# One choice of experts per batch, the threshold ahead of constants, and raised lengths in the planner of an attention and mixture-of-experts kernel

## The chip, the cores and the metric

The kernel runs on one core of a Trainium2 chip. The metric is the device time of one execution, in microseconds (us). Of the kernel before, three runs took 615.66, 617.41 and 619.67 us; the median is 617.41 us.

## The reference

Attention over 4 batches of 8 heads, with 576 rows of 64 elements in each, feeds a layer of 8 experts. A score counts only if it lies within `tau` of its row's largest.

```
scores = scale * np.matmul(q, k.transpose(0, 1, 3, 2))
thresh = np.max(scores, axis=-1, keepdims=True) - tau
scores = np.where(scores >= thresh, scores, -1000000000.0)
...
attn = attn / (np.sum(attn, axis=-1, keepdims=True) + 1e-09)
...
x = attn_out.transpose(0, 2, 1, 3).reshape(2304, 512)
logits = x @ w_gate                      # 512 x 8
expert_idx = np.argmax(logits, axis=1)
gate_w = softmax(logits)[n, expert_idx]
for i in range(N):                       # first come, first served: capacity 576 per expert
    if counts[e] < capacity: disp[e, counts[e]] = x[i]
...
h = np.maximum(np.einsum('ecd,edf->ecf', disp, w1), 0.0)     # w1 512 x 1024
y = np.einsum('ecf,efd->ecd', h, w2)                          # w2 1024 x 512
out[i] = gate_w[i] * y[expert_idx[i], pos[i]]                 # 0 where not kept
```

## The kernel before, in words

**Tiling.** The 32 heads are worked as 16 pairs, four pairs to a batch. A head's 576 rows are four blocks of 128 and a tail of 64 (`TAIL`). For each pair q and k are loaded, scaled and split into a high and a low half of 16 bits (L773 on ACT, L780 on POOL, the first pair's L782 on DVE) and transposed by DMA. TensorE computes the scores `s` (L846), DVE takes row maxima (L873, L875), TensorE computes the transposed scores `d` (L846), ACT the exponential (L938), DVE keeps what is above the threshold (L942), ACT makes the high half (L908), POOL the low half (L912), and TensorE multiplies by v (L958, L970) into `xo`. ACT copies that to `xs` (L985), DVE forms the reciprocal `rc` of the sums (L991, L992), and POOL scales the rows into `xr`, and those of the tail into `xrt` (L1006). For the x = 0 and x = 1 heads of a pair this covers 128 rows at a time, for x = 2 (both tails) 64.

**Gating.** It is done when a batch's fourth pair is done, and twice: for the four groups of 128 rows (index 0), then for the tail (index `NJ` = 4; its 128 partitions hold two halves of 64 rows). Each time DVE finds the largest logit (`gate1`, L1086, L1087), ACT the exponentials (L1094), DVE the choice of expert `oh` (L1099 to L1104), TensorE the rank of each row within its expert (L1111 to L1118), and DVE the running count `cum` (L1122), the row's metadata (`meta`, L1128 to L1135), and the row index `ixi` to write to (`gate2`, L1140 to L1151). POOL then writes the rows to `xd` in DRAM with indirect DMAs (L1157), four and then one. The next pair's work is mixed in between.

**Experts.** After the third batch the first eight tiles (one to an expert) can be gathered (L364, `earlyy`). After the fourth, the counts are summed (`tot`, L488), a chain of small DVE operations (L491 to L603, among them `gix` L579) finds out which expert each of 13 more tiles belongs to, and POOL gathers these (`latey`). A tile is transposed (`x0`, L373), split (ACT L376, DVE L381), multiplied by w1 (`A`, L399 early, L406 late), passed through the rectifier (L424, L428) and multiplied by w2 (`B`, L445); the results are scaled (L635, L639) and written (L642). The weights are loaded into `ws` (L318) and split by ACT (L329, L331, L332) and by DVE (L336) or POOL (L334).

**What sets the order.** A planner in the kernel (`Plan`) holds every task with an engine, a length in ns, what it waits for, and a priority. It simulates the engines and each time starts the best task that can begin within a window; tasks in `urgent` are taken within another (`HOLD`). The result is a fixed order of instructions for each engine, and each engine runs its own in that order. A task's length thus changes no work, only the order. The tasks `xm`, `xt`, `ta`, `gate1`, `scat` and `tot` of the code are the operations above.

## Time and profile before

| what | value |
|---|---|
| median of three runs | 617.41 us |
| profiled execution | 614.46 us |
| its span | 612.4 us |
| PE busy | 529.5 us, 86% of the span |
| DVE busy | 433.5 us, 71% |
| POOL busy | 446.6 us, 73% |
| ACT busy | 396.5 us, 65% |

The span is the profiled part of the execution; 2.06 us of its 614.46 us lie outside. Busy shares are means over a program with three parts: the attention pairs up to about 350 us, a passage from the last pair to the experts, and the experts from about 390 us on. A table by stretches shows which engine is full in each part.

### The profile page before, as it was taken

Reading aid. Unit: us, or ns where it says so; the run is one execution under the profiler, and the core shown is the slowest. Engines: PE = TensorE matmul, PEld = TensorE weight load, DVE = VectorE, ACT = ScalarE, POOL = GpSimd, SP = SyncE. Lnnn points to the kernel's source line nnn. Section 1 sums busy time; section 2 is a strip of 40 time slices with the busy share of each in tenths; the row PEclk is TensorE's granted clock in tenths of the full one; section 3 lists DMA queues with packets and bytes.
Section 4 is the critical chain, followed back from the end, with each engine's and each line's share of the span. In section 5 each row is a group of like instructions: output and inputs, shape, how many; then the busy total and the mean of one; then the engine's idle time right before and its main releaser. Section 6 shows DMA issues by size and latency. Waiting matters only on the chain.

```text
span 612.4 us, 16304 instructions
## 1 busy us (share of the span) xinstructions
PE 529.5 (86%) x6122; PEld 343.0 (56%) x6122; DVE 433.5 (71%) x999; ACT 396.5 (65%) x551; POOL 446.6 (73%) x382
## 2 busy tenths in 40 slices
PE   2868889887998979997687868699999999999993
PEld 1334545554664646665466744575774687468651
DVE  5886787889897899887776895355555555555652
ACT  5585887897897869896378755356676547625400
POOL 5365967878997689897499446308998868956864
PEclk9897999999999999998798988899999999999997
DMA  6967775578777686872152868754497529643952
GB/s 142 167 123 152 137 155 106 130 105 190 123 151 138 103 205 117 139 106 70 60 155 91 294 190 256 201 65 138 172 232 201 167 84 266 193 169 78 209 179 102
DMA packets 165327, 92.80 MB, mean 152 GB/s; under 512 B 141172, under 2 KB 153528, under 8 KB 165243
## 3 DMA queue, kind: packets, MB, share of 16 engines
q1 hardware_dynamic: 152458, 49.59, 43.0%
q0 software_dynamic: 12352, 41.80, 21.1%
q8 instruction: 53, 0.87, 0.6%
q10 hardware_dynamic: 432, 0.30, 0.2%
q14 instruction: 32, 0.25, 0.1%
HBM read 53.25 MB, written 10.24 MB: 104 GB/s over the span
## 4 chain that ended last, share of the span: by engine, by line
PE 61%; DVE 13%; DMA 11%; ACT 6%; POOL 4%; issue 3%; another core or an unknown queue 1%; SPq 0%; POOLq 0%; ACTq 0%; DVEq 0%
PE b L406 12%; PE s L846 7%; DMA qT<-qn 6%; PE d L846 6%; PE b L399 6%; PE gp L445 6%; PE xo L445 6%; PE xo L958 6%; PE b L445 5%; DVE mx L873 3%; PE xo L970 3%; DMA out_dram<-latey,oix 2%; DVE w2b L942 2%; DVE w1b L942 2%; POOL p L912 2%
## 5 line engine op out<-in xcount | busy, mean ns | idle before, releaser
L873 DVE TENSOR_REDUCE mx<-s 128x1 f32<-128x512 f32 x144 | 95.4, 680 | 26.6 <-PE s L846 25.9
L846 PE MATMUL s<-kT,qT 128*128 128x512 f16 (+2 forms) x576 | 95.8, 306 | 21.1 <-DMA qT<-qn 8.3
L846 PE MATMUL d<-qT,kT 128*128 128x512 f16 (+2 forms) x576 | 88.5, 305 | 10.4 <-DVE w1b L942 4.2
L406 PE MATMUL b<-w1b,latex 128*128 (+2 forms) x816 | 80.7, 276 | 6.9 <-ACT latex L376 3.2
L331 ACT ACTIVATE ws<-ws 128x1024 f32<-128x1024 f32 x48 | 50.5, 1051 | 47.7 <-DMA ws<-in_moe_w_dram 47.7
L406 PEld LDWEIGHTS <-latex 128*128 128x128 f16 (+1 forms) x816 | 63.1, 103 | 23.2 <-issue 6.5
L942 DVE SCALAR_TENSOR_TENSOR w2b<-d,ntau,w2b 128x1024 f32<-128x1024 f32 x56 | 71.4, 1275 | 5.0 <-ACT w2b L938 4.7
L334 POOL TENSOR_TENSOR w1b<-ws,w1b 128x1024 f16<-128x1024 f32 x24 | 51.2, 2142 | 29.8 <-ACT w1b L332 29.6
L912 POOL TENSOR_TENSOR p<-w2b,p 128x1024 f16<-128x1024 f32 x33 | 70.5, 2144 | 2.6 <-DMA qr<-in_q_dram 1.5
L334 POOL TENSOR_TENSOR w2b<-ws,w2b 128x1024 f16<-128x1024 f32 x24 | 51.0, 2137 | 20.5 <-ACT w2b L332 20.3
L938 ACT ACTIVATE w2b<-d 128x1024 f32<-128x1024 f32 x56 | 57.1, 1019 | 12.5 <-PE d L846 12.2
L846 PEld LDWEIGHTS <-qT 128*128 128x128 f16 (+1 forms) x640 | 34.9, 102 | 53.7 <-issue 25.4
L846 PEld LDWEIGHTS <-kT 128*128 128x128 f16 (+1 forms) x640 | 36.6, 101 | 49.9 <-issue 31.1
L445 PEld LDWEIGHTS <-lateh 128*128 128x128 f16 (+1 forms) x408 | 30.7, 103 | 33.8 <-issue 0.8
L958 PEld LDWEIGHTS <-p 128*128 128x128 f16 x1056 | 41.9, 99 | 11.3 <-POOL p L912 1.8
L399 PEld LDWEIGHTS <-w1b 128*128 128x128 f16 x768 | 43.9, 98 | 6.9 <-issue 5.4
L399 PE MATMUL b<-earlyx,w1b 128*128 128x128 f16 x768 | 47.1, 219 | 0.0
L958 PE MATMUL xo<-vH,p 128*128 128x65 f16 x704 | 45.2, 196 | 1.7 <-POOL p L912 1.7
L958 PE MATMUL xo<-vL,p 128*128 128x64 f16 x352 | 41.9, 193 | 0.4 <-issue 0.4
L332 ACT ACTIVATE w2b<-ws 128x1024 f16<-128x1024 f32 x24 | 25.4, 1057 | 21.2 <-PE gp L445 20.6
L318 POOL DMA_DIRECT2D ws<-in_moe_w_dram x50 | 37.4, 751 | 1.2 <-POOL w2b L334 0.9
L908 ACT ACTIVATE p<-w2b 128x1024 f16<-128x1024 f32 x33 | 34.7, 1056 | 0.4 <-DVE w2b L942 0.4
(250 smaller groups left out, 1228.6 us busy)
## 6 DMA issues: line engine op xcount, KB each, us to landing
ws<-in_moe_w_dram POOLq DMA_DIRECT2D x50, 512.0 KB
ws<-in_moe_w_dram SPq DMA_DIRECT2D x14, 512.0 KB
kr<-in_k_dram SPq DMA_DIRECT2D x16, 256.0 KB
qr<-in_q_dram SPq DMA_DIRECT2D x15, 256.0 KB
v<-in_v_dram SPq DMA_DIRECT2D x28, 128.0 KB
kr<-in_k_dram SPq DMA_DIRECT2D x32, 16.0 KB
v<-in_v_dram POOLq DMA_DIRECT2D x4, 128.0 KB
qr<-in_q_dram SPq DMA_DIRECT2D x30, 16.0 KB
```

The lines of the kernel that those rows point to most:

```text
L318: eng.dma_start(out=t, in_=src)
L331: nc.scalar.activation(out=t, in_=t, func=AF.Copy, scale=W_SCALE)
L334: nc.gpsimd.tensor_tensor(out=dst[:, :, 1, :], in0=t, in1=dst[:, :, 0, :], op=ALU.subtract)
L399: nc.tensor.matmul(out=hp[:, f * P:(f + 1) * P], lhsT=wb[0][:, o:o + P], rhs=xT[t][:, xi], start=(d == 0 and z == 0), stop=(d == NB - 1 an ...
L406: nc.tensor.matmul(out=hp[m, 0:FC], lhsT=xT[t][:, xi, m], rhs=wb[0][:, bass.ds(r + (2 * d + wi) * FC, FC)], start=(d == 0 and z == 0), sto ...
L445: nc.tensor.matmul(out=yp[m], lhsT=h[:, o, hi, m], rhs=wb[1][:, bass.ds(r + wi * DM, DM)], start=(z == 0), stop=(z == len(ops) - 1),)
L846: nc.tensor.matmul(out=out, lhsT=l, rhs=r, start=(z == 0), stop=(z == 1), **kw)
L873: V.tensor_reduce(out=m[:, i, 0:1], in_=ps_s[i % 2], axis=AX.X, op=ALU.max)
L912: eng.tensor_tensor(out=p[:, 1], in0=x, in1=p[:, 0], op=ALU.subtract)
L938: nc.scalar.activation(out=t, in_=d, func=AF.Exp, scale=sc_s)
L942: V.scalar_tensor_tensor(out=t, in0=d, scalar=ntau, in1=t, op0=ALU.is_ge, op1=ALU.mult)
L958: nc.tensor.matmul(out=ps_x[:, j * DV:j * DV + r.shape[-1]], lhsT=l, rhs=r, start=(z == 0), stop=(z == len(ops) - 1))
```

## The change

The gating of a batch is done once, with the tail as a fifth group (`NG` = 5): one `gate1`, one choice, one burst of ranks, one `gate2`, and then the five scatters. The tail's transposes and logits come ahead of the last pair's `xt`. `tot` adds the last batch's choices by two further matmuls, and needs only the ranks. The threshold `tau` is handled ahead of most constants and memsets, which become tasks of the planner behind it. The scaling of the x = 2 rows runs on 128 partitions for the later two pairs of a batch, with two small buffers more. A table `FIT` raises planned lengths, five scatters count 1300 instead of 1040, and further tasks are urgent, with priorities ahead of all others. From the diff:

```diff
-    LAND = {"load": 560, "turn": 960, "rows": 2000, "move": 1030, "gather": 980}
+    LAND = {"load": 560, "tau": 2100, "load0": 2300, "turn": 960, "rows": 2000, "move": 1030, "gather": 980}
+    FIT = dict(
+        e={1030: 908, 200: 105}, h16={560: 523, 1030: 948}, hik={1170: 1050}, hiq={1170: 1050}, sck={650: 572}, scq={650: 668},
...
+        m={600: 1280}, max={690: 597, 200: 130}, p={1280: 1190, 200: 190}, r={200: 290}, choice={637: 790, 680: 850}, meta={500: 540, 750: 870},
+        gate1={302: 280, 330: 345}, gate2={650: 860, 900: 1175}, cum={146: 280}, first1={75: 130}, first2={550: 930}, nhi={420: 570}, own={600: 920}, row={150: 260},
...
     def add(self, key, eng, dur, fn, deps, prio, dma=None, kind=None):
+        n = key[0]
+        dur = max(dur, self.FIT.get(n, {}).get(round(dur), dur))
...
-    V.memset(cum, 0.0)
-    V.memset(wg, 0.0)
-    V.memset(zero, 0.0)
...
+    def more_consts(i):
+        if i == 0:
+            V.memset(cum, 0.0)
...
     def emit_tot():
-        nc.tensor.matmul(out=ps_g[:, 512 - E:], lhsT=ones, rhs=cum, start=True, stop=True)
+        oh = gst["oh"]
+        nc.tensor.matmul(out=ps_g[:, 512 - E:], lhsT=ones, rhs=cum, start=True, stop=False)
+        nc.tensor.matmul(out=ps_g[:, 512 - E:], lhsT=ones, rhs=oh[:, NJ + 1], start=False, stop=False)
+        nc.tensor.matmul(out=ps_g[:, 512 - E:], lhsT=ones[0:TAIL], rhs=oh[0:TAIL, NJ], start=False, stop=True)
...
-        xss = [right.tile([P, NJ, D + 2], F32, name=f"xs{i}") for i in range(3)]
+        xss = [right.tile([P, NJ if i < 2 else 2, D + 2], F32, name=f"xs{i}") for i in range(4)]
...
+                if a >= HH // 2:
+                    i, rows = 2 + a % 2, slice(0, P)
+                    t, r1 = xss[i][:, 0:2], rcs[i][:, 1, 0:2]
...
+        def emit_choice(b):
+            V.scalar_tensor_tensor(out=t2, in0=t0, scalar=0.0, in1=dsc(NG, P), op0=ALU.is_equal, op1=ALU.mult)
             V.tensor_reduce(out=fe, in_=t2, axis=AX.X, op=ALU.max)
+            V.tensor_tensor(out=oh[:, 0:NG], in0=dsc(NG, P), in1=bc(fe, NG, P), op=ALU.is_equal)
...
+        T(("pad", 1), "V", 800, lambda: pads(1), [("tau",)], -59)
+        T(("pad", 2), "V", 400, lambda: (pads(2), small_pads()), [("tau",)], -30)
+        T(("const", 0), "V", 1500, lambda: more_consts(0), [("tau",)], -12)
+        T(("const", 1), "V", 1000, lambda: more_consts(1), [("const", 0)], -11)
...
-            T(("ta", qi), "P", 216, partial(emit_turn, b, NJ, 0), [("xm", s - i, 2) for i in range(HH)] + [("lge", b, 1)], t)
-            T(("logit", b, NJ), "P", 756, partial(emit_logit, b, NJ), [("tb", qi), ("gate2", b, 0)], t)
+            T(("ta", b), "P", 216, partial(emit_turn, b), [("xm", s - i, 2) for i in range(HH)] + [("xb", s - 1, 1)], t - 1)
+            T(("logit", b, NJ), "P", 756, partial(emit_logit, b), [("tb", b), ("lwg",)] + last("gate2", b - 1), t - 1)
+            T(("gate1", b), "V", 330, partial(emit_gate1, b), [("logit", b, 0), ("logit", b, NJ)], t)
+            T(("choice", b), "V", 680, partial(emit_choice, b), [("gate1", b)], t)
+            T(("rank", b), "P", 260, partial(emit_rank, b), [("choice", b)] + last("cum", b - 1), t)
+            if b < B - 1:
+                T(("cum", b), "V", 146, partial(emit_cum, b), [("rank", b)], t)
+            T(("gate2", b), "V", 900, partial(emit_gate2, b), [("rank", b), ("meta", b), ("cap",)] + ([("first1",)] if b == B - 2 else []), t)
...
-        T(("tot",), "P", 10, emit_tot1, [("cum", g, NJ), ("gate2", g, NJ)], pt)
+        T(("tot",), "P", 10, emit_tot1, [("rank", g)], pt)
...
+        plan.urgent |= {("av", NPR - 1, x, j) for x in range(3) for j in range(NJ)} | {(n, NPR - 1, c) for n in ("h16", "l16") for c in range(5)}
+        HX = {(n, 0, t) for n in ("h1", "h2") for t in range(NE)}
+        plan.urgent |= HX
+        for k in plan.urgent:
+            if k in plan.tasks:
+                t = plan.tasks[k]
+                plan.tasks[k] = t[:4] + (t[4] / 1000 - (700 if k in HX else 600 if k[0] in ("gate1", "gexp", "choice", "rank", "meta", "gate2", "scat") else 500),) + t[5:]
```

The first place is POOL around the third batch's gating, before: L1157 are the scatters of the four groups (`xr`) and of the tail (`xrt`), L912 low halves of the next pair, L1006 scalings, L794 the low half of v.

```order
L912 TENSOR_TENSOR w1b<-w2b,w1b 128x1024
L1157 DMA xd<-xr,ixi 18432x514 x3
L1006 TENSOR_TENSOR xr<-xs_196,rc_199 128x4x64
L1157 DMA xd<-xr,ixi 18432x514
L912 TENSOR_TENSOR p_160<-w2b,p_160 128x1024
L1157 DMA xd<-xrt,ixi 36864x257
L912 TENSOR_TENSOR p_161<-w2b,p_161 128x1024
L912 TENSOR_TENSOR w1b<-w1b 128x512
```

The same place now (L1171 scatters, L935 low halves, L1033 scalings, L817 v):

```order
L935 TENSOR_TENSOR w1b<-w2b,w1b 128x1024
L1033 TENSOR_TENSOR xr<-xs_180,rc_184 128x4x64
L817 TENSOR_TENSOR vL_151<-v_157,vH_148 128x640
L935 TENSOR_TENSOR p_144<-w2b,p_144 128x1024
L935 TENSOR_TENSOR p_145<-w2b,p_145 128x1024
L935 TENSOR_TENSOR w1b<-w1b 128x512
L1171 DMA xd<-xr,ixi 18432x514
L1171 DMA xd<-xrt,ixi 36864x257
L1171 DMA xd<-xr,ixi 18432x514 x3
```

The five scatters stand in one block, behind three low halves, the scaling and the split of v.

The second place is POOL at the last pair, before (L364 gathers of early tiles, L1006 the last pair's scalings, L1157 the last batch's scatters, L318 loads of weights):

```order
L912 TENSOR_TENSOR p_163<-w2b,p_163 128x1024
L364 DMA earlyy<-xd,gie 128x514 x4
L1006 TENSOR_TENSOR xr<-xs_195,rc_198 128x4x64
L364 DMA earlyy<-xd,gie 128x514
L1006 TENSOR_TENSOR xr<-xs_196,rc_199 128x4x64
L1006 TENSOR_TENSOR xrt<-xs_197,rc_200 64x128
L1157 DMA xd<-xr,ixi 18432x514 x4
L318 DMA ws<-in_moe_w_dram 128x2x512
L1157 DMA xd<-xrt,ixi 36864x257
L318 DMA ws<-in_moe_w_dram 128x2x512
L318 DMA ws<-in_moe_w_dram 128x4x256 x2
L364 DMA latey<-xd,gix 128x514 x6
```

and now (L380 gathers, L1033 scalings, L1171 scatters, L334 loads):

```order
L935 TENSOR_TENSOR p_147<-w2b,p_147 128x1024
L1033 TENSOR_TENSOR xrt<-xs_181,rc_185 128x128
L1033 TENSOR_TENSOR xr<-xs_179,rc_183 128x4x64
L380 DMA earlyy<-xd,gie 128x514 x3
L1033 TENSOR_TENSOR xr<-xs_180,rc_184 128x4x64
L1033 TENSOR_TENSOR xrt<-xs_182,rc_186 128x128
L380 DMA earlyy<-xd,gie 128x514 x3
L1171 DMA xd<-xr,ixi 18432x514
L1171 DMA xd<-xrt,ixi 36864x257
L1171 DMA xd<-xr,ixi 18432x514 x3
L334 DMA ws<-in_moe_w_dram 128x2x512
L380 DMA latey<-xd,gix 128x514 x4
```

The last pair's scaling has no gather in front of it, and one load of weights instead of four lies between the last batch's first scatter and the late gathers.

The third place is DVE in the last batch's gating, before, from the four groups' `gate2` on (L336 splits of w2, L428 and L381 work for early tiles, L491 the first operation of the chain behind `tot`; after these rows the tail's choice, count, metadata and `gate2` follow with four further L336 between them):

```order
L1151 TENSOR_TENSOR ixi<-sm 128x4
L336 SCALAR_TENSOR_TENSOR w2b<-ws,w2b 128x512
L428 SCALAR_TENSOR_TENSOR earlyh<-b_5152,earlyh 128x256
L428 SCALAR_TENSOR_TENSOR earlyh<-b_5153,earlyh 128x256
L1086 TENSOR_REDUCE sm<-gp 128x1
L1087 TENSOR_TENSOR tb<-gp,sm 128x8
L336 SCALAR_TENSOR_TENSOR w2b<-ws,w2b 128x512
L1099 SCALAR_TENSOR_TENSOR tb<-tb,desc 128x8
```

and now (L444 and L397 early tiles, L510 the chain's first, L352 the splits of w2):

```order
L1159 TENSOR_TENSOR ixi<-sm 128x4
L1161 TENSOR_TENSOR sm<-sm 128x1
L1162 TENSOR_SCALAR ixi<-sm,half 128x1
L444 SCALAR_TENSOR_TENSOR earlyh<-b_5157,earlyh 128x256
L510 SCALAR_TENSOR_TENSOR most<-gp,cap_f,fst 128x8
...
L621 TENSOR_TENSOR gix<-own 64x4
L622 TENSOR_TENSOR bad<-own,bl 64x4
L352 SCALAR_TENSOR_TENSOR w2b<-ws,w2b 128x512 x9
```

From `gate1` to the chain's end no split of w2 is left on DVE; nine of them follow behind it.

## Rows read from the trace of the kernel before

**Rows 1.** The page's first part: engine, busy us, share of the span, instructions.
```profile
PE 529.5 (86%) x6122; PEld 343.0 (56%) x6122; DVE 433.5 (71%) x999; ACT 396.5 (65%) x551; POOL 446.6 (73%) x382
```
**Rows 2.** Busy us by stretch: length, engines, granted clock, DMA share, GB/s; cut at pairs' L875.
```profile
126.00:151.00 25.00, 20.21 (x286) 13.05 (x286) 22.86 (x66) 20.24 (x32) 18.85 (x17) 1.00 0.72 148
151.00:168.70 17.70, 15.17 (x223) 9.85 (x222) 14.72 (x32) 14.84 (x22) 17.65 (x15) 1.00 0.76 133
276.70:308.90 32.20, 24.46 (x318) 15.62 (x311) 24.78 (x73) 15.85 (x25) 19.87 (x18) 0.84 0.18 54
...
360.00:400.00 40.00, 27.82 (x162) 17.66 (x162) 22.67 (x89) 15.62 (x31) 22.45 (x24) 0.87 0.75 209
...
460.00:520.00 60.00, 60.00 (x554) 39.31 (x553) 34.42 (x66) 36.23 (x35) 47.96 (x35) 1.00 0.69 183
```
**Rows 3.** Timeline of the start, ACT and DVE: start, length, instruction, idle before and releaser.
```profile
6.96 1.25 ACT L773 ACTIVATE qn<-qr,g 128x1152 f16<-128x1152 f32 x1 [4.65 <-DVE g L296]
6.78 0.15 DVE L296 TENSOR_SCALAR g<-tau_t 128x1 f32<-128x1 f32 x1
```
**Rows 4.** The chain that ended last, first piece: start, length, what.
```profile
1.28 4.25 DMA kr<-in_k_dram
```
**Rows 5.** Timeline of DVE in the third batch's gating.
```profile
281.73 1.27 DVE L1099 SCALAR_TENSOR_TENSOR tb<-tb,desc 128x32 f32<-128x32 f32 x1
283.25 1.82 DVE L1101 TENSOR_TENSOR oh<-desc,sm 128x32 f16<-128x32 f32 x1
...
293.13 2.47 DVE L1099 SCALAR_TENSOR_TENSOR tb<-tb,desc 128x8 f32<-128x8 f32 x1
```
**Rows 6.** Timeline of POOL in the same stretch.
```profile
282.91 2.12 POOL L912 TENSOR_TENSOR w1b<-w2b,w1b 128x1024 f16<-128x1024 f32 x1
287.99 1.03 POOL L1157 DMA_INDIRECT xd<-xr,ixi  x1 [2.97 <-DVE ixi L1151]
...
293.44 2.13 POOL L912 TENSOR_TENSOR p<-w2b,p 128x1024 f16<-128x1024 f32 x1
303.33 0.99 POOL L1157 DMA_INDIRECT xd<-xrt,ixi  x1 [7.76 <-DVE ixi L1149]
```
**Rows 7.** All scatters (L1157): POOL's idle time before them by releaser, us and times.
```profile
  DVE ixi L1149: 8.7, 2
  DVE ixi L1151: 5.4, 3
```
**Rows 8.** Timeline of DVE and POOL at the last pair.
```profile
340.88 0.18 DVE L992 RECIPROCAL rc<-rc 128x4 f32<-128x4 f32 x1
341.58 0.63 POOL L1006 TENSOR_TENSOR xr<-xs,rc 128x256 f32<-128x256 f32 x1
343.45 0.98 POOL L1006 TENSOR_TENSOR xr<-xs,rc 128x256 f32<-128x256 f32 x1
```
**Rows 9.** Timeline of DVE in the last batch's gating.
```profile
353.94 0.18 DVE L1086 TENSOR_REDUCE sm<-gp 128x4 f32<-128x32 f32 x1
354.26 0.68 DVE L336 SCALAR_TENSOR_TENSOR w2b<-ws,w2b 128x512 f16<-128x512 f32 x1
354.86 0.18 DVE L1099 SCALAR_TENSOR_TENSOR tb<-tb,desc 128x32 f32<-128x32 f32 x1
```
**Rows 10.** Timeline of POOL from the last batch's scatters to the late gathers.
```profile
359.17 1.05 POOL L1157 DMA_INDIRECT xd<-xr,ixi  x1 [9.81 <-DVE w2b L336]
...
365.14 1.03 POOL L1157 DMA_INDIRECT xd<-xrt,ixi  x1 [0.30 <-DVE over L620]
370.60 1.07 POOL L364 DMA_INDIRECT latey<-xd,gix  x1 [2.09 <-DVE ex L585]
```
**Rows 11.** Timeline of PE and ACT at the first late tiles.
```profile
374.19 1.46 PE L445 MATMUL b<-w2b,earlyh 128*128 128x512 f16 x6
379.01 1.67 PE L406 MATMUL b<-w1b,latex 128*128 x12 [1.21 <-issue]
389.33 0.38 ACT L424 ACTIVATE hw<-b 128x256 f16<-128x256 f32 x1 [5.17 <-remote]
```

More of the change, by code (lines that the diff above doesn't have):

```diff
@@ L975, in xs_of @@
         def xs_of(s, x):
-            i = (3 * s + x) % 3
+            i = x if x < 2 else 2 + s % HH % 2
             if x < 2:
@@ L1144, in emit_gate2 @@
             )
-            V.tensor_tensor(out=ix, in0=ix, in1=rk, op=ALU.add)
-            if j:
-                V.tensor_tensor(out=dp, in0=ix, in1=dp, op=ALU.add)
-                V.tensor_scalar(out=ixi[:, 0:G], in0=dp, scalar1=2.0, scalar2=half[:, 0:1], op0=ALU.mult, op1=ALU.add)
-            else:
-                V.tensor_tensor(out=ixi[:, 0:G], in0=ix, in1=dp, op=ALU.add)
-            gst[b, j] = (G, n, xrows[b][0 if j == 0 else 1], ixi)
+            for j in (0, NJ):
+                gst[b, j] = (xrows[b][0 if j == 0 else 1], ixi[:, j:])
@@ L1399, in attention_moe_kernel @@
         g = B - 1
[L1400 removed]
+        plan.urgent |= {(n, g) for n in ("gate1", "gexp", "choice", "rank", "meta", "gate2", "ta", "tb")} | {("logit", g, NJ)}
+        plan.urgent |= {("scat", g, 0, r) for r in range(NJ)} | {("scat", g, NJ, 0)} | {(n, g, h) for n in ("lgt", "lge", "lgs") for h in range(2)}
         if PR["urg"] > 0:
```

291 lines of the change are left out of this document (141 added, 150 removed).

## The prediction, made before the changed kernel was run

> **What bounds the kernel now.** I read the page first: PE is busy 86% of the span, no other engine above 73% [rows 1]. That is a mean, so the table of stretches came next [rows 2]. From 460 to 520 us PE is busy 60.00 of 60 us at full clock; such is the whole part of the experts behind its first tiles, and the change leaves that part's matmuls alone. Time can come only from what lies before. There the table shows three kinds of stretch. A pair within a batch takes 17.7 us, with POOL busy 17.65 of it: nothing to take. A pair in which a batch is gated takes 25.0 us (126 to 151; the first two boundaries are alike), with DVE the fullest at 22.86. The third boundary takes 32.2 us, in which no engine is busy above 24.78 and the DMA share is 0.18: there engines wait for each other. And from 360 to 400 us PE is busy only 27.82 of 40. Then I read the timelines of those places, and the waits before POOL's scatters.
>
> **The change, part by part.** The sum is made against the profiled execution, 614.46 us, of which 2.06 lie outside its span. The median of the runs, 617.41, stands 2.95 above it, and I add that at the end.
>
> *Start.* ACT's first scaling waits 4.65 us for `g`, and `g` stands on DVE behind constants and memsets at 6.78 although `tau` was requested first [rows 3]. With those moved behind it, the next thing late is the load: the first chain piece is a load of k in flight from 1.28 to 5.53 [rows 4]. So the gain lies between 0 (later pairs absorb it) and 6.96 - 5.53 = 1.4. The moved operations fall into DVE's idle time before scores exist; if that is not enough they cost what they gave. I take -1.0, near the upper end, because nothing else feeds the first scaling.
>
> *Gating once.* Per batch DVE issues 22 small operations in place of 34 (20 in the last). Two such rows take 354.26 - 353.94 = 0.32 us, or 0.16 each [rows 9], so 12 of them are 1.9 us, on the engine that is fullest at a boundary. The five-group rows are a quarter wider and DVE had 2.1 us idle in the 25.0, so I take -1.2 at each of the first two boundaries: -2.4 (bounds 0 and -3.8). The two more matmuls of `tot` and the longer burst of ranks fall where PE waits for DVE anyway.
>
> *Third boundary.* Here three operations of the two choices took 1.27, 1.82 and 2.47 us [rows 5] where the same take 0.18 in the last batch [rows 9]. Each ends just behind a POOL addition (283.25 + 1.82 = 285.07 against 282.91 + 2.12 = 285.03; 295.60 against 295.57 [rows 5, 6]): they wait for POOL, 5.0 us in all. POOL in turn stood 2.97 and 7.76 us at the scatters for `ixi` [rows 6], with the next pair's low halves behind it in its queue. With one choice and one block of scatters there is one such circle instead of two. The excess over the first boundary is 32.2 - 25.0 = 7.2, and with the 1.2 from above 8.4; I leave one wait of 2.1 behind a POOL addition in the new choice and take -6.3 (bounds 0 and -8.4). The cover is what now stands ahead of the scatters on POOL: three low halves, a scaling and the split of v.
>
> By the Trainium skill (SBUF — State Buffer, section "SBUF: two separate sides"), VectorE and GpSimd share a pair of SBUF ports under an exclusive lock, so that a VectorE operation with two SBUF inputs waits out a GpSimd operation that reads SBUF. The three rows agree with it; by that rule alone the wait belongs to neighbours and not to the number of groups, and the term would be about 2 us smaller with a second wait.
>
> *Last pair.* The second `xr` starts at 343.45 although its `rc` was done at 341.06; ahead of it in POOL's order stand gathers and the first `xr`, at 341.58 [rows 8]. Now the first scaling comes ahead of the gathers and the second waits only for `rc`: up to -2.4. `xt`, the logits and `gate1` hang on it; I take -2.0. The tail's scaling on 128 partitions costs the same columns as on 64; I cost it at nothing.
>
> *From `gate1` to the first late product.* Call G the start of the last `gate1`, 353.94. Before, product A of tile 8 starts at 379.01, G + 25.1 [rows 9, 11]. Twelve splits of w2 lay between on DVE, each 0.60 (354.26 to 354.86), together 7.2, and a second pass of gating; none is left. Reading the new order with the old lengths, `ixi` is ready at about G + 4.6; five scatters at 1.03 + 0.30 [rows 10] end at G + 11.3, against 366.17 = G + 12.2. The first gather came 4.4 us after the last scatter, part of it waiting for the DVE chain. It now starts between G + 11.3 and G + 15.7; I take G + 13.8, against G + 16.7: -2.9. Of four loads of weights between scatters and gathers one is left; with the DMA share at 0.75 and 209 GB/s over this stretch [rows 2], three loads of 512 KB would be 7 us of traffic, and I take -2.0 for the gathers' landing (bounds 0 and -7). That puts the product at G + 20.2, -4.9. The nine splits now behind the chain end at about G + 18.5 and hold B of the early tiles back; one B, 1.46 [rows 11], goes behind as filler and is paid later. Net -3.5 (bounds +2 and -9).
>
> *Raised lengths and new priorities.* They add no work but reorder every engine in every pair. A pair's 17.7 us are POOL's 17.65, so order can hardly gain; where a wait is placed badly it can cost some tenths per pair. I cost it at 0, bounds -3 and +5 (0.3 over 16 pairs).
>
> Sum: -1.0 - 2.4 - 6.3 - 2.0 - 3.5 = -15.2, so 599.3 for a profiled execution, and with 2.95 **602.2 us** for the median. By its own bounds this case runs from 597 to 608. Chance 0.42.
>
> **Rivals.** *More: ACT's stall goes.* At 389.33 ACT had stood 5.17 us before a rectifier, for something the profile calls remote [rows 11]; the chain of rows names no engine of this core. If it hangs on the exact moment or on the traffic there, the shifted order may lose it: 602.2 - 5.2 = 597. Against it: no edit touches what it waited for, as far as the rows show. Chance 0.24.
>
> *Absorbed.* The gain at boundaries is not there: pairs are paced by POOL and DVE's total, and the four groups now wait for the tail's x = 2 rows, so that the early half of the gating no longer overlaps. Then only the start and the passage after G remain: -4.5, which gives 612.9. For it: the first two boundaries have only 1.9 us idle on DVE per 25 to win from. Chance 0.17.
>
> *Slower: POOL's queue blocks at every boundary.* At the first two boundaries all waits for `ixi` together were small: 8.7 - 7.8 = 0.9 for the tail, and of the four groups 5.4 - 3.0 = 2.4 [rows 6, 7]. With the tail in the same `gate2`, the block of five scatters stands on POOL until the tail's logits are done, as the single tail scatter did for 7.76. Two boundaries at 7.8 in place of 3.3 together: +12.3, with no gain at the third, and the start, the passage and the last pair as forecast: 614.5 + 12.3 - 1.0 - 3.5 - 2.0 = 620.3, and 623 to 628 with the 2.95 and a loss by the new order. It decides where the tail's logits come later than POOL's rows ahead of the block, at the third boundary two low halves of 2.1 and a scaling of 0.6 [rows 6, 8], 4.8 us, and two smaller operations; that cover speaks against it. Chance 0.10.
>
> *The new order itself.* Pairs within batches grow by 0.3 us or more each and eat a good part of the 15: 606 to 616. Chance 0.07.
>
> **The numbers.** This kernel's runs spread over 0.65%, so a change under about 1% can't be told from none; the bounds are 611.2 and 623.6. Forecast, ACT's stall, half of the absorbed case, and half of the last one are faster: 0.42 + 0.24 + 0.07 + 0.03 = 0.76. The rest of those two and the lower edge of the slower case are the same: 0.14. Slower: 0.10. The range reaches from 591 (ACT's stall gone and the upper bounds at the boundaries) to 615 (the absorbed case): it leaves out the slower rival and the far low end.
>
> **What would show it.** In the profile after: the first q scaling on ACT at 5.5 to 6, not 7; boundaries of about 24, 24 and 26 us between successive L875 rows, with one wait of POOL before the first scatter of a batch and none before the tail's; choice operations at 0.2, or at most one at 2; the last `gate1` about 12 us earlier than 353.94, from the four terms ahead of it; tile 8's product 20 us after it; then dense PE to the end, as long as before. I am wrong if the pairs within a batch take 18 us or more, if POOL stands over 5 us before each batch's scatters, or if B of the early tiles waits for the nine splits so long that tile 8 comes at G + 25 again.

## The result and the profile after

| kernel | median | runs | before beside it | ratio to before, 95% interval |
|---|---|---|---|---|
| changed | 623.44 us (620.28 to 628.17) | 4 | 616.93 us, 4 runs | 1.0127 [1.0087, 1.0167] |

The change made the kernel 1.3% slower. Forecast were 602.2 us, in a range of 591 to 615, with a chance of 0.10 for slower: the forecast was wrong. The profiled execution took 620.28 us with a span of 618.3, against 614.46 and 612.4. Ratios here and below leave out runs that were over 1.5% above the fastest of their kernel (a slower state); the medians do not.

The page's first part, in the columns of [rows 1]:
```profile
PE 532.3 (86%) x6128; PEld 348.1 (56%) x6128; DVE 432.2 (70%) x950; ACT 398.9 (65%) x547; POOL 447.3 (72%) x382
```
No engine has much more to do (DVE's 49 instructions fewer are the second choice that is gone). What changed is who waits. Stretches of the changed kernel, in the columns of [rows 2]; the cuts are the third boundary (276.77 to 304.93), the last pair up to the last `gate1` (L1101, which I call G, as in the prediction), and the 46.65 us behind G:
```profile
276.77:304.93 28.16, 22.75 (x316) 15.78 (x313) 21.98 (x60) 13.12 (x22) 17.29 (x14) 0.94 0.18 55
304.93:355.45 50.52, 39.30 (x531) 31.40 (x531) 39.59 (x70) 36.75 (x65) 33.37 (x25) 0.83 0.59 189
355.45:402.10 46.65, 30.27 (x243) 21.34 (x242) 24.66 (x98) 17.32 (x36) 22.66 (x23) 0.85 0.58 162
```
The third boundary is 4 us shorter than in [rows 2], the last pair is 5.4 us longer (50.52 against 353.94 - 308.86 = 45.08), and behind G PE works only 30.27 of 46.65 us.

The timeline from the scatters to the first late tiles, of POOL, ACT and PE:
```profile
365.66 0.97 POOL L1171 DMA_INDIRECT xd<-xr,ixi  x1 [0.30 <-issue]
372.76 0.78 POOL L334 DMA_DIRECT2D ws<-in_moe_w_dram  x1 [6.13 <-issue]
373.84 1.06 POOL L380 DMA_INDIRECT latey<-xd,gix  x1 [0.31 <-issue]
...
390.35 1.01 POOL L380 DMA_INDIRECT latey<-xd,gix  x1 [0.30 <-issue]
```
```profile
366.86 0.38 ACT L440 ACTIVATE earlyh<-b 128x256 f16<-128x256 f32 x1 [3.25 <-remote]
392.69 0.38 ACT L440 ACTIVATE hw<-b 128x256 f16<-128x256 f32 x1 [6.57 <-remote]
```
```profile
372.22 0.59 PE L461 MATMUL gp<-w2b,earlyh 128*128 128x512 f16 x1 [7.58 <-DVE w2b L352]
381.18 1.47 PE L422 MATMUL b<-w1b,latex 128*128 x12
394.10 2.83 PE L422 MATMUL b<-w1b,latex 128*128 x12 [5.03 <-ACT hw L440]
```
POOL stands 6.13 us before the one load of weights that was left between scatters and gathers, and all gathers stand behind it. (The row names no releaser. The split of w2 that the load waits for is read from the kernel's dependencies; the first one behind the chain ran on DVE from 371.48, and PE's product that needs it began 0.54 us before the load.) ACT stands twice here for something "remote", where [rows 11] had one such stand of 5.17, and PE stands behind ACT. The last row is also dear in itself: twelve products of 128 columns took 2.83 us there and 1.47 at 381.18. From 392.31 to 399.14 us the granted clock was 0.5 (1.2 GHz), after PE's idle time; at 381 it was 1.0 (2.4 GHz).

**What "remote" is.** The trace also records when each semaphore is raised. I paired the ends of PE's signalling instructions with those records. In the profile of before 582 pairs have a median lag of 0.014 us, but 19 came over 0.4 us late; in the changed kernel it is 32 of 592, up to 8.27 us. Of the 32, 27 overlap the issue of an indirect DMA on POOL (scatters, gathers, outputs), and 4 more begin within 0.6 us of the end of one; of the 19 of before 17 overlap, and 2 begin within 0.6 us. The two stands of ACT above fit two of these signals: matmuls that ended at 363.57 and 384.40 were seen at 366.84 and 392.67, and ACT began 0.02 us later. So PE had finished, and ACT learned of it 3.3 and 8.3 us later. Between 110 and 320 us, where the first three batches' scatters lie, the lags of before sum to 12.3 us (8 signals), those of the changed kernel to 31.2 us (16 signals).

Of ACT, DVE and POOL no signal that has a record came late in either profile. But of the changed kernel's signals 49 have no record (19 of DVE, 18 of ACT, 10 of PE, 2 of POOL), and 47 of these ended in the same places, during or within 0.6 us of an indirect DMA of POOL. So it is not shown that the lag is PE's alone, nor that the recording has no part in it.

### The profile page after: what moved, and what is told of

Read it like the earlier page. It is cut to its first block, busy times and chain, and to the rows that moved or that the text cites. A ratio compares the mean times of both kernels' runs of the same rounds, so it can differ in the third digit from the quotient of the medians.

```text
span 618.3 us, 16259 instructions
## 1 busy us (share of the span) xinstructions
PE 532.3 (86%) x6128; PEld 348.1 (56%) x6128; DVE 432.2 (70%) x950; ACT 398.9 (65%) x547; POOL 447.3 (72%) x382
## 3 DMA queue, kind: packets, MB, share of 16 engines
q1 hardware_dynamic: 152458, 49.59, 40.7%
## 4 chain that ended last, share of the span: by engine, by line
PE 56%; DVE 14%; DMA 12%; POOL 6%; ACT 5%; issue 5%; another core or an unknown queue 1%; SPq 0%; POOLq 0%; DVEq 0%; ACTq 0%
PE b L422 11%; PE d L869 7%; PE s L869 7%; PE b L415 7%; PE xo L981 5%; PE xo L461 5%; PE gp L461 4%; PE b L461 4%; DMA qT<-qn 4%; DVE w2b L965 3%; DMA out_dram<-latey,oix 2%; DVE mx L896 2%; POOL p L935 2%; DVE w1b L352 2%; DMA kT<-kn 2%
## 5 line engine op out<-in xcount | busy, mean ns | idle before, releaser
L869 PE MATMUL d<-qT,kT 128*128 128x512 f16 (+2 forms) x576 | 87.1, 307 | 8.9 <-DVE w2b L965 4.4
L935 POOL TENSOR_TENSOR p<-w2b,p 128x1024 f16<-128x1024 f32 x33 | 70.7, 2147 | 6.5 <-ACT p L931 6.0
L334 POOL DMA_DIRECT2D ws<-in_moe_w_dram x50 | 37.4, 751 | 20.8 <-DVE w2b L352 13.4
L415 PE MATMUL b<-earlyx,w1b 128*128 128x128 f16 x768 | 48.9, 222 | 3.3 <-DVE earlyx L397 3.3
L981 PE MATMUL xo<-vH,p 128*128 128x65 f16 x704 | 47.2, 199 | 4.9 <-POOL p L935 2.8
L981 PE MATMUL xo<-vL,p 128*128 128x64 f16 x352 | 43.3, 196 | 1.0 <-issue 1.0
L444 DVE SCALAR_TENSOR_TENSOR hw<-b,hw 128x256 f16<-128x256 f32 x52 | 22.1, 424 | 20.7 <-ACT hw L440 16.2
```

The source lines that it names most:

```text
L334: eng.dma_start(out=t, in_=src)
L415: nc.tensor.matmul(out=hp[:, f * P:(f + 1) * P], lhsT=wb[0][:, o:o + P], rhs=xT[t][:, xi], start=(d == 0 and z == 0), stop=(d == NB - 1 an ...
L869: nc.tensor.matmul(out=out, lhsT=l, rhs=r, start=(z == 0), stop=(z == 1), **kw)
L935: eng.tensor_tensor(out=p[:, 1], in0=x, in1=p[:, 0], op=ALU.subtract)
L981: nc.tensor.matmul(out=ps_x[:, j * DV:j * DV + r.shape[-1]], lhsT=l, rhs=r, start=(z == 0), stop=(z == len(ops) - 1))
```

## The experiments

Runs were made in five later sittings, each with its own runs of before. Only ratios are compared across sittings. In the first three, every profile shows late signals of PE (21 to 28 in each); in the last two, none does.

| sitting | kernel | median us | before us | ratio, 95% interval |
|---|---|---|---|---|
| 1 | nofit | 629.43 | 614.76 | 1.0222 [1.0156, 1.0288] |
| 1 | noprio | 630.90 | 614.76 | 1.0261 [1.0215, 1.0306] |
| 1 | loadsp | 625.28 | 614.76 | 1.0166 [1.0103, 1.0230] |
| 1 | spaced | 623.86 | 614.76 | 1.0120 [1.0055, 1.0186] |
| 2 | beforefp | 626.36 | 615.27 | 1.0142 [1.0086, 1.0198] |
| 2 | startk | 626.91 | 615.27 | 1.0167 [1.0094, 1.0240] |
| 2 | splitwait | 618.16 | 615.27 | 1.0038 [0.9991, 1.0086] |
| 2 | tailafter | 619.04 | 615.27 | 1.0024 [0.9978, 1.0070] |
| 3 | onechoice | 631.35 | 615.08 | 1.0249 [1.0180, 1.0318] |
| 3 | spread | 611.99 | 615.08 | 0.9949 [0.9915, 0.9984] |
| 3 | both | 617.10 | 615.08 | 1.0003 [0.9966, 1.0040] |
| 3 | all4 | 615.06 | 615.08 | none given (609.33, 609.58, 620.53, 620.78) |
| 4 | blocklate | 605.52 | 604.03 | 0.9998 [0.9951, 1.0045] |
| 4 | beforespread | 622.70 | 604.03 | 1.0273 [1.0199, 1.0346] |
| 4 | splitspread | 606.10 | 604.03 | 1.0013 [0.9969, 1.0057] |
| 4 | bothspread | 615.93 | 604.03 | 1.0181 [1.0103, 1.0259] |
| 5 | again (the changed kernel) | 602.61 | 604.02 | 0.9962 [0.9928, 0.9996] |
| 5 | blocklate2 | 606.40 | 604.02 | 1.0008 [0.9966, 1.0050] |

### Parts of the change by themselves

Theories at the start: the waits that the new order makes; the one choice by itself; the lengths and priorities by themselves.

**nofit**
```diff
-    FIT = dict(...)
+    FIT = {}
```


> The changed kernel with its lengths as before (table FIT empty); all else of the change stays. Waits theory (the 1.3% are waits that the new order makes: splits of weights on DVE beside POOL's additions in the last pair, the tail's logits ahead of xt, POOL's one load of w2 that stands 6.13 us for a deferred split with the late gathers behind it): the old lengths put another order there, some splits inside the gating chain and few behind it, so the first late gather should come within 3 us of the last scatter, not 7.2, and tile 8's product near G + 21 in place of G + 25.7: about 615 to 619. Lengths theory (the raised lengths alone cost it all): 602 to 608, as I forecast for the rest of the change. One-choice theory (the gating in one piece costs by itself): 622 to 626, no different from the changed kernel.

**noprio**
```diff
-        plan.urgent |= {("av", NPR - 1, x, j) ...}
...
-                plan.tasks[k] = t[:4] + (t[4] / 1000 - ...,) + t[5:]
```


> The changed kernel without its last block, which makes the last pair's av, h16 and l16 and the early tiles' h1 and h2 urgent and raises the priorities of the urgent work. Waits theory: here three loads of w2 stand ahead of the scatters and two between scatters and gathers, and the splits lie partly inside the chain; the stand of POOL before the first late gather shrinks or goes, but the loads themselves lie in the gathers' way: 616 to 622. Lengths theory: the raised lengths are still there, so 621 to 626. One-choice theory: 621 to 626 too. Under 612 would say that the urgent priorities are the loss.

**onechoice**: both edits together.


> The changed kernel without its raised lengths and without its last block of urgent work: one choice per batch, the new start and the new tail scaling alone, on the old lengths and priorities. One-choice theory (the choice in one piece costs by itself): 622 to 630. Waits theory: the old order's luck is gone as well, since the gating in one piece moves its neighbours; 618 to 628. If the one choice gives what I forecast and only lengths and priorities eat it: 602 to 608.

**beforefp**: the kernel before with FIT and with that last block.


> The kernel before with two parts of the change alone: its raised lengths (table FIT) and its last block of urgent work and priorities. Two choices per batch, the old start and the old tail scaling stay. Taking either part out of the changed kernel cost 6 to 7.5 us, so they help there. If one choice per batch is what loses (one-choice theory), they help here as well and nothing eats it: 606 to 610, against 615 for before. If the waits of the new order lose (waits theory), they come with the lengths and priorities: 618 to 624. If neither part matters without the one choice: 614 to 617.

All four medians lie above every range given. Without the lengths, without the priorities, or without both, the changed kernel is 1 to 1.3 points slower still. On the kernel before, the same two parts cost 1.4 points. So the lengths theory falls, as far as sittings with late signals show: the two parts help one structure and cost the other. With them, two choices (1.0142) and one choice (1.0127) can't be told apart. On the old lengths and priorities one choice is 2.5% slower than two (onechoice, which has the new start and tail scaling too), so the one-choice theory stands there. None of the four was run without late signals.

### The start

**startk**
```diff
-    LAND = {"load": 560, "tau": 2100, "load0": 2300, ...}
+    LAND = {"load": 560, "tau": 2100, "load0": 560, ...}
```


> The changed kernel with one planned length altered: the first loads of q and k count 560 ns, as before, in place of 2300. That puts ACT's first k scaling back between the two q scalings; in the changed kernel ACT took both q first, stood 1.17 us for the second piece of q, and PE's first turn came at 11.03 us in place of 9.32. Expected: PE's first turn at 8.5 to 9.4, and the first mx of a pair that was at 23.91 (22.51 before) at 21.5 to 22.6. If the gain holds to the end, 621 to 622; if later pairs absorb it, 623 to 624. The rest of the order shifts too, by which 2 us either way are possible.

ACT's start in the changed kernel, and PE's first turns there and in startk:
```profile
6.24 1.26 ACT L796 ACTIVATE qn<-qr,g 128x1152 f16<-128x1152 f32 x1 [3.93 <-DMA qr<-in_q_dram]
8.66 1.26 ACT L796 ACTIVATE qn<-qr,g 128x1152 f16<-128x1152 f32 x1 [1.17 <-DMA qr<-in_q_dram]
9.83 2.21 ACT L796 ACTIVATE kn<-kr 128x1152 f16<-128x1152 f32 x2
11.03 2.10 PE L830 MATMUL d<-ident,kn 128*128 128x128 f16 x18 [11.03 <-ACT kn L796]
```
```profile
8.74 2.10 PE L830 MATMUL d<-ident,kn 128*128 128x128 f16 x18 [8.74 <-ACT kn L796]
14.94 0.39 PE L869 MATMUL s<-kT,qT 128*128 128x512 f16 x1 [2.90 <-DVE qT L837]
```
The threshold does come early (the first scaling is at 6.24, before at 6.96 [rows 3]). But the longer planned load puts both pieces of q ahead of k, and PE's first turn at 11.03 against 9.32 before. Putting the length back brings that turn to 8.74, but the scores then wait for q; the first L898 moves only from 23.91 to 23.50 (L875 before: 22.51), and the end shows nothing of it (1.0167 of before).

### The last pair

**splitwait**
```diff
-  partial(split_w, i, e, 1, z, of), [("w0", z) + me], pw)
+  partial(split_w, i, e, 1, z, of), [("w0", z) + me] + ([("l16", NPR - 1, 4)] if me < (0, 0, 2) else []), pw)
```


> The changed kernel with DVE's splits of w1 for the first two experts held until the last pair's last low half is done, so that no split with two SBUF operands runs beside POOL's additions there; one load of weights slides behind the late gathers. Waits theory: the split that took 5.51 us at 328.22 takes 0.7, earlyx comes 2 to 3 us earlier, the last gate1 is 2 to 3 us earlier than in the changed kernel: 620 to 621.5. One-choice theory: the pair waits for other things, 623 to 624.

**tailafter**
```diff
-                if a == HH - 1 and i == 0:
-                    free.append(("tb", b))
...
-            T(("ta", b), ..., [("xm", s - i, 2) ...] + [("xb", s - 1, 1)], t - 1)
+            T(("ta", b), ..., [("xm", s - i, 2) ...] + [("lge", b, 1)], t)
```


> The changed kernel with the tail's turn and logits behind the logits of the four groups on PE, as before, and the turn of the gated rows no longer behind the tail's. In the changed kernel the second xr ended at 342.65 and its turn began only at 345.37, 2.7 us later, as PE stood for the tail's xr and xgT. Waits theory: the turn follows its xr within 0.2 us, but the one gating now waits for the tail at the end of the logits, which costs 1 to 2 of it: last gate1 1 to 2 us earlier, 621.5 to 622.5. One-choice theory: the tail is waited for wherever it stands, 623 to 626.

**both**: these two together.


> The changed kernel with both repairs of the last pair: DVE's splits of the first two experts held until the last low half is done, and the tail's turn and logits behind the groups' logits. POOL's load then stands behind the late gathers by itself. Each alone gave 4 to 6 us (618.2 and 619.0 against 623.4). If they mend different waits: 612 to 615, with the last gate1 5 to 7 us earlier than in the changed kernel. If both mend the same wait: 617 to 619.

What splitwait takes away, in DVE's and POOL's timeline of the changed kernel:
```profile
328.22 5.51 DVE L352 SCALAR_TENSOR_TENSOR w1b<-ws,w1b 128x512 f16<-128x512 f32 x1
334.11 0.69 DVE L397 SCALAR_TENSOR_TENSOR earlyx<-b,earlyx 128x512 f16<-128x512 f32 x1
...
336.52 0.68 DVE L352 SCALAR_TENSOR_TENSOR w1b<-ws,w1b 128x512 f16<-128x512 f32 x1
```
```profile
327.85 1.07 POOL L380 DMA_INDIRECT earlyy<-xd,gie  x1
328.96 4.21 POOL L935 TENSOR_TENSOR p<-w2b,p 128x1024 f16<-128x1024 f32 x2
333.13 0.85 POOL L1033 TENSOR_TENSOR xrt<-xs,rc 128x128 f32<-128x128 f32 x1
```
A split of 0.68 us took 5.51, beside POOL's issue of a gather, its two additions and the start of its scaling. It ended at 333.73; 0.68 us earlier, at 333.05, is about where the additions ended (333.17); PE's early products waited 2.01 us for the `earlyx` behind it. The Trainium skill (SBUF — State Buffer, section "SBUF: two separate sides") has such an exclusive lock between the two engines, for a VectorE operation with two SBUF inputs against a GpSimd operation that reads SBUF. The row agrees in that the split does not end beside the additions. By the Trainium skill the operation that starts first gets the ports, and this the rows don't bear out: the split is shown from 328.22, the first addition from 328.96. In splitwait the stretch from the last L898 to G takes 352.40 - 306.98 = 45.42 us, 5.1 less, and before's 45.08 are back. The median gained about as much (one load also slid behind the late gathers there). tailafter's gain is not where the repair aimed: in its profile (of a run of 627.9 us, its slowest) the same split takes 6.36 us, the last pair 49.58, and G comes at 356.85, later than in the changed kernel. So its median is better than expected for a reason that was not found. Both repairs together (1.0003) give no more than either (1.0038, 1.0024).

### What stands between scatters and gathers

**loadsp**
```diff
-            gather=-4.39, lw0=-5.19, out=2, hold=70, k2=6, ws0=-12.48,
+            gather=-4.39, lw0=-5.19, out=2, hold=70, k2=8, ws0=-12.48,
```


> The changed kernel with one number altered (8 for 6), by which the two loads of w2 that POOL issues near its late gathers are issued by SP. POOL's late gathers then follow the scatters with no load between. Waits theory: the 6.13 us for which POOL stood before the load go; the first late gather moves from G + 18.4 to G + 13 or 14, tile 8's product from G + 25.7 by up to 4.5 us; since B of the early tiles still waits for the deferred splits, a half of that is gained: 619 to 622, 618.5 at the best. One-choice or lengths theory: unchanged, 623 to 624.

**spaced**: loadsp, and
```diff
-               ... + ([("own",)] if t >= NE + NF else []) + land, ...)
+               ... + ([("own",)] if t >= NE + NF else []) + ([("x0", t - 3)] if t > NE + 2 else []) + land, ...)
...
-  T(("lw",) + me, "G", 1081, ..., [("swap",)] + free, pl, ...)
+  T(("lw",) + me, "G", 1081, ..., [("swap",), ("gather", NS - 1)] + free, pl, ...)
```


> As the kernel with both loads on SP, and each late gather from the fourth on also waits until the tile three before it has landed, so that POOL does not issue its indirect DMAs in one unbroken series. It asks what holds PE's semaphore signals: in both traces they are seen 0.014 us after a matmul's end, but 2 to 8 us late during such series, and ACT stood 6.57 us at 392.69 for one of them. If the unbroken series holds them, signal lags over 2 us among the late gathers go, ACT's stand falls under 1 us, and PE's idle time from 373 to 395 shrinks by 2 us or more; against that the last gathers come 1 to 3 us later, which the early products cover: 617 to 621. If something else holds them (traffic, the clock), the lags stay and the time is that of the loads on SP, 619 to 624.

The stand of 6.13 us goes (3.60 in loadsp), and from G to the end the profiles take 258.8 and 258.0 us in place of 262.85. The medians do not follow: G itself came 8 us later, at 363.6 and 364.2, with a second boundary of 30.3 and 29.3 us (26.6 in the changed kernel) and a third of 31.7 us in both profiles, where ACT or DVE stood 2.6 to 5.7 us, most of it for late signals. Among the late gathers the longest lag fell from 4.0 us (loadsp) to 2.7 (spaced) and ACT's stand from 4.49 to 2.41. But spaced did not do what its edit was meant to do. Its late gathers still stand one behind the other, 0.30 us apart as in loadsp:
```profile
386.50 1.26 POOL L380 DMA_INDIRECT latey<-xd,gix  x1 [0.30 <-issue]
388.06 1.01 POOL L380 DMA_INDIRECT latey<-xd,gix  x1 [0.30 <-issue]
```
So what gaps between gathers do to the lags was not tested, and these two runs say little of the load, either.

### The block of scatters

**spread**
```diff
-  n + PR["scat"] + r / 4, dma=...
+  n + PR["scat"] + (r / 4 if b == B - 1 else 2 + 2 * r if b == B - 2 else 4 + 4 * r), dma=...
```


> The changed kernel with the scatters of the first three batches spread over the following pair or two (2 to 4 steps of a pair's nine apart) in place of one block of five behind each other. In the changed kernel PE's signals reach ACT and DVE 2 to 5 us late during such a block; on the kernel with the splits held back ACT stood 5.57 us at 301.39 and DVE 5.52 us at 302.23 for them. If the block of scatters holds the signals: lags over 0.4 us fall from 18 in the three boundaries to 6 or fewer, the third boundary takes 25 to 28 us in place of 28 to 33, the first two 23 to 25, and the end comes 3 to 7 us earlier: 616 to 620. If something else holds them: lags and time stay, 622 to 625.

**all4**: spread, loadsp, splitwait and tailafter.


> The kernel with both repairs, and also with both early loads of w2 issued by SP and with the scatters of the first three batches spread. If the signals held by blocks of scatters are a cost of their own: 606 to 611, faster than before's 615. If not: 612 to 616, as with the two repairs alone.

Spread is the only kernel of the first three sittings that is faster than before. Its edit touches the planned places of fifteen scatters alone; the order of the other work shifts with them. The third boundary on POOL, first in the changed kernel, then spread:
```profile
301.01 0.97 POOL L1171 DMA_INDIRECT xd<-xr,ixi  x1 [0.30 <-issue]
302.29 0.97 POOL L1171 DMA_INDIRECT xd<-xr,ixi  x1 [0.30 <-issue]
303.28 0.41 POOL L1033 TENSOR_TENSOR xrt<-xs,rc 64x128 f32<-64x128 f32 x1
...
305.56 2.13 POOL L935 TENSOR_TENSOR p<-w1b,p 128x1024 f16<-128x1024 f32 x1 [1.30 <-ACT p L931]
```
```profile
295.50 0.97 POOL L1171 DMA_INDIRECT xd<-xr,ixi  x1 [0.30 <-issue]
296.50 2.13 POOL L935 TENSOR_TENSOR p<-w1b,p 128x1024 f16<-128x1024 f32 x1
...
299.71 1.02 POOL L1171 DMA_INDIRECT xd<-xr,ixi  x1 [0.17 <-issue]
```
The three boundaries take 21.68, 23.42 and 26.06 us, together 71.2, against 23.56 + 26.60 + 28.16 = 78.3 in the changed kernel. The lags between 110 and 320 us sum to 11.1 us, not 31.2 (10 signals against 16: less than half in sum, but not the 6 or fewer that I expected). The spreading itself is partial: at the second boundary three scatters still follow each other (216.26 to 218.85), at the third four (291.63 to 295.50).

This leaves at least two causes: signals held while a block of scatters is issued, or low halves that stand behind the block in POOL's queue; and the order that shifted with the edit can't be set apart from either.

**blocklate**, and the same kernel as **blocklate2**
```diff
-  n + PR["scat"] + r / 4, dma=...
+  n + PR["scat"] + (r / 4 if b == B - 1 else 8 + r / 100), dma=...
```


> The changed kernel with the five scatters of a batch kept behind each other but put eight steps later, behind four or more of the next pair's low halves. If POOL's queue is the cost (the next pair's low halves standing behind five scatters): the gain of the spread kernel stays, 611 to 614. If the signals that PE sends are held while a block of scatters is issued: the lags come again, 2 to 5 us, wherever the block stands, and the time is 618 to 624.

> The changed kernel with the block of five scatters behind four or more of the next pair's low halves, which was 0.9998 of before on a chip without late signals. If this chip shows late signals and they are the cost of a block wherever it stands: 1.005 to 1.015. If POOL's queue is the cost: 0.995 to 1.002 on either sort of chip, and at least 0.010 below the changed kernel beside it. On a chip without late signals, a distance under 0.004 to the changed kernel says that the queue costs nothing.

**again**: the changed kernel itself, beside blocklate2.


> The changed kernel itself, as it was timed first (1.0127 of before). If this chip shows late signals of PE: 1.010 to 1.016 again. If it shows none, and the late signals were what the change lost: 0.99 to 1.002 of before. If it shows none and the change loses by its order and by POOL's queue alone: 1.010 to 1.016 all the same.

blocklate's edit did not keep the five together. At the third boundary of blocklate2 low halves run between them (the program is the same in blocklate):
```profile
296.28 1.02 POOL L1171 DMA_INDIRECT xd<-xr,ixi  x1 [0.57 <-DVE sm L1161]
298.86 1.14 POOL L935 TENSOR_TENSOR w1b<-w1b 128x512 f16<-128x512 f32 x1 [1.56 <-ACT w1b L931]
300.17 1.00 POOL L1171 DMA_INDIRECT xd<-xrt,ixi  x1 [0.16 <-POOL w1b L935]
...
303.74 2.14 POOL L935 TENSOR_TENSOR p<-w1b,p 128x1024 f16<-128x1024 f32 x1
306.96 1.02 POOL L1171 DMA_INDIRECT xd<-xr,ixi  x1 [0.16 <-ACT xs L1008]
```
So it is another way of spreading: it relieves POOL's queue, but it could not have shown whether a block holds signals wherever it stands.

Sittings 4 and 5 happened to show no late signal at all: 0 of 602 over 0.4 us in again, with the same program and the same DMAs, and 1 signal without a record in place of 49. Before took 604.0 us there (42 runs) in place of about 615, and the changed kernel 602.6 in place of 623.4. I could not have built this experiment, and I did not control it either: what differs between the sittings is not known. The work itself agrees in the two traces of the program: POOL is busy 446.3 us in again and 447.3 in the first profile, and the packets of the largest DMA queue take 42.3% of 597.5 us = 252.7 and 40.7% of 618.3 us = 251.7. Without late signals the changed kernel is 0.4% faster than before, at an interval that just clears 1; and blocklate2 beside it, with the queue relieved, is not faster but, if anything, slower. So where no signal is late, POOL's queue costs nothing that relieving it gives back; with late signals that was not run. The same stretches of again:
```profile
274.40:298.72 24.32, 21.57 (x312) 14.97 (x308) 21.97 (x60) 13.39 (x22) 14.86 (x11) 0.93 0.13 35
298.72:348.35 49.63, 36.55 (x539) 28.98 (x536) 39.34 (x69) 36.48 (x65) 35.72 (x29) 0.93 0.63 206
348.35:395.00 46.65, 39.67 (x346) 28.07 (x344) 31.34 (x111) 23.48 (x47) 23.16 (x24) 0.93 0.73 184
```
Behind G, PE works 39.67 of the same 46.65 us, at a granted clock of 0.93 in place of 0.85. POOL and PE there:
```profile
358.57 0.97 POOL L1171 DMA_INDIRECT xd<-xr,ixi  x1 [0.30 <-issue]
362.56 0.77 POOL L334 DMA_DIRECT2D ws<-in_moe_w_dram  x1 [3.02 <-issue]
363.64 1.07 POOL L380 DMA_INDIRECT latey<-xd,gix  x1 [0.31 <-issue]
```
```profile
362.03 0.58 PE L461 MATMUL gp<-w2b,earlyh 128*128 128x512 f16 x1 [4.48 <-DVE w2b L352]
371.08 1.74 PE L422 MATMUL b<-w1b,latex 128*128 x12
373.09 1.47 PE L422 MATMUL b<-w1b,latex 128*128 x12
374.84 1.65 PE L422 MATMUL b<-w1b,latex 128*128 x12
```
Half of the stand before the load is gone (3.02 for 6.13), because the chain of small operations on DVE is no longer held up 3.00 us behind ACT's late `earlyh`. The late products follow each other without the stands of 1.83 and 5.03, and no row of ACT or DVE between 60 and 560 us names a remote releaser. What stays is the last pair: 49.63 us, with the same split of 5.51 us in it (at 321.19). So that cost is not one of late signals.

**beforespread**: the same edit of the scatters on the kernel before.


> The kernel before, two choices per batch, with its scatters of the first three batches spread in the same way. Its lags were 8 in the three boundaries, up to 2.9 us, and its third boundary took 32.2 us with 7.76 us of POOL standing before the tail's scatter. If the block of scatters is what costs there as well: 608 to 612. If it costs only in one piece of five, or the old order holds its gain by other things: 613 to 617.

**splitspread**: spread and splitwait.


> The spread kernel (612.0) with DVE's splits of the first two experts held until the last low half is done. The last pair of the spread kernel, from its last mx of 512 columns to the last gate1, took 54.6 us against 45.4 with the splits held in the changed kernel. If that stretch is shortened by 4 us or more here as well: 606 to 609. If the spread kernel's later pairs have already taken that gain: 611 to 613.

**bothspread**: spread, splitwait and tailafter.


> The spread kernel with both repairs of the last pair, the loads of w2 as in the changed kernel. The kernel with four edits had its last gate1 at 347.8, 6 us ahead of before, and gave 609.3 in its two better runs. If the loads on SP were what disturbed that kernel: 606 to 609. If the repairs shift the order so that other waits grow: 611 to 616.

The ranges expected in sitting 4 were set from times with late signals, so that splitspread's 606.1 lies in one of them is chance. Without late signals no kernel gained by spreading: beforespread loses 2.7%, its three boundaries take 28.15, 28.17 and 29.29 us. splitspread shortens the last pair to 43.6 us as expected but takes 260.3 from G to the end, where again takes 249.2, and ends no better than before. Nothing here shows that a repair is worth anything where no signal comes late; I did not run splitwait or spread alone there.

## Why the prediction was wrong

The steps of the sum against the profile of before (which has late signals), in us:

| step | forecast | changed kernel, late signals | again, no late signals |
|---|---|---|---|
| start (first L875, now L898) | -1.0 | +1.4 | +2.1 |
| first two boundaries | -2.4 | -1.3 + 1.3 = 0.0 | -3.2 + 0.6 = -2.6 |
| third boundary | -6.3 | -4.1 | -7.9 |
| pairs between | 0 | -1.2 | -1.8 |
| last pair up to G | -2.0 | +5.4 | +4.6 |
| G to the end | -3.5 | +4.4 | -9.3 |
| sum | -15.2 | +5.9 | -14.9 |

- **The terms that failed.** The last pair (-2.0 forecast, +5.4 measured) and the stretch behind G (-3.5, +4.4) have the wrong sign and make up 15.3 of the 21.1 us between the two sums. For the last pair I took G to follow the earlier scaling; what set it was the split of 5.51 us and the products that waited behind it, and with the splits held back (splitwait) the stretch is down to 45.42. Behind G I took the late product to follow the shorter chain; what set it was the load that waits for a deferred split (6.13 us), then PE's stands of 1.83 and 5.03 us behind late signals, and the lower clock behind them.
- **The step behind the second of these** is the reading of waits as a property of the order. For the third boundary I put its 7.2 us excess down to circles of small operations between DVE and POOL, of which one would go. In before's trace signals of PE came 2.0, 2.9 and 1.3 us late just there, between the scatters, and the chain to the 7.76 us of POOL's stand in [rows 6] begins with one of them: the signal of a matmul that ended at 290.23 was seen at 292.23, and the tail's `gate1` began then (the row names another product of PE; the logits that `gate1` reads are that matmul's):
```profile
292.25 0.17 DVE L1086 TENSOR_REDUCE sm<-gp 128x1 f32<-128x8 f32 x1 [2.74 <-PE xo L958]
```
  For ACT's 5.17 us [rows 11] I wrote that no edit touches what it waited for. It was a late signal: the matmul ended at 382.43, its signal was seen at 389.31, while POOL issued its series of gathers. The change touches such series, too: it gathers the scatters of a batch into one block of five, and I costed the block at nothing.
- The sum of the last column is close to the forecast by accident. It sets a kernel without late signals against a profile with them, and its terms differ from mine. Like against like the change gives +6.5 us with late signals and about -2 us without. So the forecast fails without late signals too: some 13 of its 15 us are not there, and where they went is not known but for the last pair.
- **Third boundary, the small operations** (-6.3 forecast, -4.1 measured): I kept one wait behind a POOL addition; there are two, of 1.91 and 1.82 us (L1111, L1113, at 285.51 and 287.68), where before had three. Right in kind.
- **Start**: wrong in sign. The early threshold was real, but the raised planned length of the load reordered ACT, which I did not price.
- **Last pair**: wrong in sign. The tail's first scaling does come ahead of the gathers, but a split of weights got between POOL's additions, and the tail's logits ahead of the second `xt`. It is the order's cost, not the signals': it is there in both columns.
- **G to the late product**: the chain was as short as forecast (the first scatter at G + 5.0). I named the nine deferred splits as what would hold PE's B, and it did so for 7.58 us; but I did not see that POOL's one load waits for such a split, with all gathers behind it. Tile 8 came at G + 25.7, not G + 20, which I had named as a sign of being wrong; without late signals it came at G + 22.7.
- **The rival on the slow side** gave 620.3 to 628, and the time is in it, but not by its mechanism: POOL stood 4.37, 2.14 and 1.16 us before the first three batches' scatters, not over 5.

**Open**: what holds the signals, whether the recording has a part in it, and what differs between the sittings; the record gives the same chip number for the third (late signals) and the fifth (none). I have no profile of before without late signals, so where its 11 us lie was not seen; the profiles show the lags and their place, and the runs that both kernels are faster in the sittings without them. That the lags are the cause of those 11 and 21 us is argued from their places, not shown by an edit that removes them alone.

## What to carry to other kernels

A stand that the profile calls remote, on a program with one core, was here a signal of the core itself that came late, in all three stands behind G that I followed: look at what POOL was issuing then, and don't count such a wait as something that an edit of the waiting engine can remove. A block of issues ahead of other work is not free, so give it a term in the sum. But spreading it is no rule: where signals came late it went with 0.5% faster than before in place of 1.3% slower, where none did the same edit cost the kernel before 2.7%. Compare both kernels beside each other in more than one sitting: the same change was 1.0127 in one and 0.9962 in another. And planned lengths and priorities are tuned to one structure: taken over to another, or taken away, they cost 1 to 1.4 points here, where signals came late.

## What the runs showed of the hardware

- PE's semaphore signals, 0.014 us late in the median, came up to 8.3 us late while POOL issued indirect DMAs one behind the other or within 0.6 us of one (31 of 32 in the changed kernel, 19 of 19 in before), and then several in one moment: those of matmuls that ended at 384.40, 384.83, 388.64 and 389.08 were all seen between 392.67 and 392.91. Signals of ACT, DVE and POOL that have a record did not in these two profiles; 39 of theirs in the changed kernel have none.
- In the profiles of two of six sittings there were none, and both kernels were faster: before by 11.0 us (1.8%), the changed kernel, the same program, by 20.8 us (3.3%) in the one where it was run.
- PE's idle time cost a second time, by the clock: behind the stand of 5.03 us twelve products took 2.83 us in place of 1.47, at 1.2 GHz. Worked out from the mean granted clock, some 52 of the changed kernel's 618.3 us were at 1.2 GHz (0.958), 32 of again's 597.5 (0.973), 40 of before's 612.4 (0.967). Late signals are not the only way there: blocklate2, without any, had 51 of 602.7 (0.958).
- A DVE split of weights with two SBUF inputs, 0.68 us by itself, took 5.51 us beside POOL's work in both profiles of the changed kernel (at 328.22 and 321.19), and 6.36 in tailafter.
